# A fused transformer block under a list planner: later K/V column groups wait for the fourth block, V's constant columns are filled in pieces, a fourth shift buffer, idle matmuls at more places

## The chip, the cores and the metric

One core of a Trainium2 chip. The metric is device microseconds (us) of one execution. Most kernels here were timed many times and the median is quoted; "fast runs" are those within 1.5% of the kernel's fastest, and only they are compared; of all timings here one, of pl_aus, was slow. TensorE (PE in the profile) does the matmuls, ScalarE (ACT) the exponentials, VectorE (DVE) copies, statistics and an integer form of the exponential, GpSimd (POOL) memsets and small products. Each run also lists its mean granted TensorE clock, where 1 is the full rate; a half-rate stretch is a piece of the run in which the trace shows 0.50. The tail is everything behind the last exponential. A run of heads is the four heads that are worked on together for one block of 512 queries.

## The reference

```python
# x (1, 2048, 512) bf16, 32 heads of 16, F = 1376
sa, ca, ga, sb, cb, gb = six parts of  silu(c) @ w_mod
h = layernorm(x) * (1 + ca) + sa
x = x + ga * (softmax(q k^T / 4) v) @ wo          # q, k, v = h @ wqkv
h = layernorm(x) * (1 + cb) + sb
x = x + gb * (gelu(h @ w1 + b1) @ w2 + b2)
```

The costly part is 32 heads x 2048 x 2048 exponentials. In pieces of 128 x 512 these are 2048 pieces, divided between ScalarE and VectorE.

## The kernel before

The program is not written in the order in which it runs. Every operation is an object with an engine, an estimate of its duration, its dependencies, a buffer that it takes and a priority. A planner keeps a clock of its own, and at each step puts down the operation that can start first on some engine (`commit`). The order on every engine is thus fixed when the kernel is built, and it depends on all estimates, priorities and buffer counts together.

```python
A_US = {1: 0.49, 2: 0.92, 3: 1.345}          # planner's estimate of an exponential of 1, 2, 3 pieces
r_ph = res("ph", 3, [P, 4 * QB], I16)        # buffers of VectorE's integer exponential
...
def dyn(plan, o):                            # priority on PE, smaller goes first
    ...
    if o.due <= prog():
        return 2.5 + same                    # work that is overdue
...
def step(self):                              # one step of the planner
    ...
    if h is not None:                        # h: a matmul on zeros, only to keep TensorE busy
        hs = max(self.start(h), self.cool)
        end = hs + h.us + 0.11
        if hs <= nxt and (not pe or pe[0][0] >= end or hs < HEAT_MIN):
            self.commit(hs, self.add(h))
```

These idle matmuls come whole (one of 128 x 512 into a spare bank) or in sets of four (onto the accumulator of the running head, adding zero). V carries constant columns, filled once by GpSimd:

```python
def v_init(b):
    def go(o):
        for t in range(b * TPB, (b + 1) * TPB):
            for ph in (range(NPH) if t in DKS else (0,)):
                v = v_tile(t, ph)
                nc.gpsimd.memset(v[:, 32 * VW:32 * VW + 15], 0.0)
                nc.gpsimd.memset(v_cols(v)[:, :, 16:17], PH_W[ph])
    return op("POOL", go, 1.5, prio=1.0 + b)
...
for cc in range(1, NC):                      # column groups 2 to 4 of K and V
    for b in range(NQ):
        make_k(b, cc, f"c{cc}", r_ax, "DVE")
        make_v(b, cc, f"c{cc}", r_ax, "DVE")
```

The softmax here doesn't subtract the row's maximum and nothing guards it: scores larger than these inputs give would overflow.

## Time and profile before

| | before |
|---|---|
| first timing | 804.71 us, median of 3 (801.36 to 807.18) |
| profiled run | span 800.8 us, mean clock 0.992 |
| PE / VectorE / ScalarE / GpSimd busy | 733.3 / 742.8 / 763.6 / 96.9 us |
| exponentials on ScalarE / integer pieces on VectorE | 634 instructions / 464 |
| first, fourth, seventh exponential start | 17.43, 21.86, 29.12 us |
| last exponential ends; tail behind it | 774.73; 26.03 us |

The two counts stand for one division of the 2048 pieces: 464 for VectorE, 1584 for ScalarE in instructions of two or three pieces. The lines themselves are in the prediction.

### The profile page before, as it was taken

What the parts mean: (1) busy time and instruction counts of PE and PEld (TensorE: products, weight loads), DVE (VectorE), ACT (ScalarE), POOL (GpSimd) and SP (SyncE); (2) the same over time, 40 slices, a digit from 0 to 9 for tenths busy, and PEclk for the clock granted to TensorE, in tenths of its full rate; (3) what the DMA queues carried; (4) which work ended last, traced back from release to release, by engine and by line L of the source; (5) the groups of instructions that cost most, each with busy time, mean ns of one, the idle gap of its engine ahead of it and who ended that gap; (6) DMA issues with size and microseconds to landing.
All of it is one profiled execution on the core that took longest, in us unless ns stands there. A gap on an engine that the chain in (4) does not pass through costs nothing. (4 is left out here: it accounts for less than half of the span.)

```text
span 800.8 us, 20101 instructions
## 1 busy us (share of the span) xinstructions
PE 733.3 (92%) x8146; PEld 273.7 (34%) x8223; DVE 742.8 (93%) x1292; ACT 763.6 (95%) x691; POOL 96.9 (12%) x241
## 2 busy tenths in 40 slices
PE   7889999989998999899988999999999999989997
PEld 3433323332222332222322332232233344434454
DVE  7779899989999999799999999999999999999975
ACT  2999999999999999999999999999999999999993
POOL 4422302100002000000001100000000100020100
PEclk9999999999999999999999999999999999999999
DMA  6115000102100000010100000011100001000010
GB/s 211 54 35 156 18 16 19 36 16 67 39 18 15 20 15 17 11 28 25 42 16 19 16 10 12 23 23 29 45 16 19 4 19 43 18 16 25 24 43 28
DMA packets 34199, 26.22 MB, mean 33 GB/s; under 512 B 15005, under 2 KB 29502, under 8 KB 34106
## 3 DMA queue, kind: packets, MB, share of 16 engines
q1 hardware_dynamic: 33578, 24.94, 11.0%
q8 instruction: 64, 1.05, 0.5%
q14 instruction: 29, 0.24, 0.1%
q10 hardware_dynamic: 528, 0.00, 0.0%
HBM read 21.30 MB, written 2.61 MB: 30 GB/s over the span
## 5 line engine op out<-in xcount | busy, mean ns | idle before, releaser
L802 ACT ACTIVATE pt<-st 128x1536 bf16<-128x1536 f32 x634 | 721.0, 1304 | 10.4 <-PE st L753 6.8
L843 DVE TENSOR_SCALAR ph<-ax 128x512 int16<-128x512 f32 x464 | 303.0, 681 | 16.9 <-PE ax L753 15.4
L858 DVE TENSOR_SCALAR sh<-ph 128x2048 int16<-128x2048 int16 x464 | 304.5, 696 | 0.7 <-PE od L891 0.3
L753 PE MATMUL st<-qm,kT 32*128 32x512 bf16 x1584 | 248.8, 384 | 30.8 <-ACT pt L802 24.1
L753 PEld LDWEIGHTS <-kT 32*128 32x128 bf16 x2048 | 83.6, 91 | 256.0 <-issue 247.0
L891 PE MATMUL od<-sh,VX 128*32 128x512 bf16 (+1 forms) x2336 | 164.7, 342 | 5.9 <-DVE sh L858 4.9
L753 PE MATMUL ax<-qm,kT 32*128 32x512 bf16 x464 | 161.4, 380 | 9.0 <-DVE ph L843 5.6
L891 PE MATMUL od<-pt,VEB 128*32 128x512 bf16 (+1 forms) x1976 | 147.2, 342 | 1.0 <-ACT pt L802 0.8
L891 PEld LDWEIGHTS <-VEB 128*32 128x32 bf16 x2560 | 62.1, 96 | 82.1 <-issue 69.1
L891 PEld LDWEIGHTS <-VX 128*32 128x32 bf16 x2336 | 57.7, 95 | 82.0 <-issue 71.0
L943 POOL TENSOR_TENSOR OT<-OD,RB 128x256 bf16<-128x256 f32 x38 | 28.7, 763 | 326.0 <-DVE sh L858 222.7
L891 PE MATMUL od<-ph,VEB 128*32 128x512 bf16 (+1 forms) x584 | 48.4, 342 | 1.4 <-DVE OD L916 0.9
L943 POOL TENSOR_TENSOR OS<-OD,RB 128x256 bf16<-128x256 f32 x24 | 17.2, 727 | 196.9 <-DVE sh L858 117.7
L1106 PE MATMUL ax<-blk,W 128*128 128x512 bf16 (+1 forms) x128 | 34.7, 368 | 1.4 <-issue 0.5
L644 PE MATMUL ax<-blk,w 128*128 128x512 bf16 x92 | 30.8, 386 | 4.1 <-issue 1.2
L1043 PE MATMUL ax<-w,g 128*128 128x512 bf16 x102 | 28.6, 381 | 2.1 <-DVE y L1087 1.0
L689 POOL TENSOR_SCALAR VX<-VEB 128x128 bf16<-128x128 bf16 x64 | 22.2, 347 | 59.0 <-DVE VEB L585 55.3
L1116 DVE TENSOR_SCALAR g<-ax,b1c 128x512 bf16<-128x512 f32 (+1 forms) x37 | 26.4, 716 | 0.3
L559 DVE BATCH_NORM_STATS2 ln_s<-xb 128x6 f32<-128x512 bf16 x32 | 21.7, 678 | 2.2 <-DMA xb<-in_A_x_dram 2.1
L1043 PEld LDWEIGHTS <-g 128*128 128x128 bf16 x176 | 14.3, 97 | 23.8 <-issue 12.4
L916 DVE COPY OD<-od 128x512 f32<-128x512 f32 x31 | 21.2, 682 | 0.7 <-issue 0.4
L1106 PEld LDWEIGHTS <-W 128*128 128x128 bf16 x176 | 14.2, 97 | 18.5 <-issue 11.4
(109 smaller groups left out, 365.9 us busy)
## 6 DMA issues: line engine op xcount, KB each, us to landing
RB<-rn SPq DMA_DIRECT2D x124, 64.0 KB
xb<-in_A_x_dram SPq DMA_DIRECT2D x8, 512.0 KB
out_dram<-o SPq DMA_DIRECT2D x16, 128.0 KB
w<-in_A_wqkv_dram SPq DMA_DIRECT2D x3, 512.0 KB
W<-in_B_w_dram SPq DMA_DIRECT2D x1, 1376.0 KB
blk<-in_w_mod_dram SPq DMA_DIRECT2D x2, 512.0 KB
xb<-in_w_mod_dram SPq DMA_DIRECT2D x2, 512.0 KB
g<-in_w_mod_dram SPq DMA_DIRECT2D x2, 512.0 KB
```

Of the source, the lines that this page charges most:

```text
L559: nc.vector.bn_stats(out=st6, in_=src)
L644: return chain([(lambda ps, j=j: nc.tensor.matmul(out=ps[:, 0:QB], lhsT=w.tile[:, j, cc * P:(cc + 1) * P], rhs=o_h[b].tile[:, j, :], start ...
L689: nc.gpsimd.tensor_scalar(out=v_cols(VX[(t, ph)])[:, 8 * cc:8 * cc + 8, 0:16], in0=v_cols(v_tile(t, 0))[:, 8 * cc:8 * cc + 8, 0:16], scala ...
L753: nc.tensor.matmul(out=o.tile[:, k * QB:(k + 1) * QB], lhsT=kT[cc][kb][rows, ko * P:(ko + 1) * P], rhs=qm.tile[rows, par, :] if hb is None ...
L802: nc.scalar.activation(out=e.tile[:, 0:len(got) * QB], in_=o.tile[:, 0:len(got) * QB], func=ACT.Exp, scale=ESC)
L843: nc.vector.tensor_scalar(out=ph.tile[:, o.row * QB:(o.row + 1) * QB], in0=o.tile, scalar1=PH_B, scalar2=0.0, op0=ALU.add, op1=ALU.max)
L858: sh = op("DVE", lambda o, j=j: nc.vector.tensor_scalar(out=o.tile, in0=first.tile, scalar1=PH_SH[j], scalar2=None, op0=ALU.add), 0.6, es, ...
L891: nc.tensor.matmul(out=o_od[r].tile[32 * i:32 * i + 32, n * HB:n * HB + w], lhsT=v_tile(kt, ph)[:, c0:c0 + 32], rhs=got[i][:, at:at + w], ...
L943: two = [op("POOL", lambda o, c=c: after_dve(nc.gpsimd.tensor_tensor(out=OT.tile[:, c * HB:(c + 1) * HB], in0=OD.tile[:, c * HB:(c + 1) * HB],
L1043: nc.tensor.matmul(out=ps, lhsT=g[:, f, col:col + P], rhs=rhs, start=(f == 0), stop=(f == NF - 1))
L1106: mm = chain([(lambda ps, f=f, j=j: nc.tensor.matmul(out=ps[:, 0:N], lhsT=W1[:, j, f * P:(f + 1) * P], rhs=h.tile[:, j, 0:N], start=(j == ...
L1116: ev.append(op("DVE", lambda o, f=f, mm=mm: nc.vector.tensor_scalar(out=g.tile[:, f, 0:N], in0=mm.tile[:, 0:N], scalar1=b1c[:, f:f + 1], s ...
```

## The change

Its intent: keep the early buffers free for the four LayerNorms by letting the column groups 2 to 4 wait for a later block's K, keep GpSimd free of memsets until the first LayerNorm has its statistics, give VectorE one more buffer, and let the idle matmuls in at more places. Two priorities change (overdue work, the LayerNorm of the block tails), and the planner's zero-length bookkeeping leaves GpSimd's list for a list of its own.

```diff
-            if hs <= nxt and (not pe or pe[0][0] >= end or hs < HEAT_MIN):
+            if hs <= nxt and (not pe or pe[0][0] >= end or pe[0][1].kind == "qkD" and hs >= self.cool):
...
-    r_ph = res("ph", 3, [P, 4 * QB], I16)
+    r_ph = res("ph", 4, [P, 4 * QB], I16)
...
-            return 2.5 + same
+            return (2.5 if o.due + 16 > prog() else 0.8) + same
...
-        return op("POOL", None, 0.0, deps, lat=0.0, prio=0.0, rel=(owner,))
+        return op("NIL", None, 0.0, deps, lat=0.0, prio=0.0, rel=(owner,))
... (the same for every other op without an instruction)
+    def v_init(v, w, prio, gate):
+        x = v[..., 0:32 * VW].rearrange("p t (h w) -> p t h w", w=VW)
+        return [op("POOL", lambda o, to=to, c=c: nc.gpsimd.memset(to, c), 0.35, prio=prio, gate=gate)
+                for to, c in ((v[..., 32 * VW:32 * VW + 15], 0.0), (x[:, :, 8:32:8, 0:15], 0.0), (x[..., 16:17], w))]
...
+        late = (lambda: True) if b == 0 else (lambda: first_ln[0])
+        o_v0[b] = v_init(VEB[b], PH_W[0], 1.0 + b, late)
...
-                   [o_sc, o_warm] + [w[0] for w in ws], kind, r_ax, [w[2] for w in ws])
+                   [o_sc, o_warm, ws[0][0]], kind, r_ax, [w[2] for w in ws],
+                   need=lambda i: ws[i // NC][0])
...
-                                    None, r_blk, ("DVE",) * 4, r_ax, kind, 1.6, None, nt)
+                                    None, r_blk, ("DVE",) * 4, r_ax, kind, 0.3, None, nt)
...
-            make_k(b, cc, f"c{cc}", r_ax, "DVE")
-            make_v(b, cc, f"c{cc}", r_ax, "DVE")
+            make_k(b, cc, f"c{cc}", r_ax, "DVE", o_k[(0, min(b + AHEAD, LAST))])
+            make_v(b, cc, f"c{cc}", r_ax, "DVE", o_k[(0, min(b + AHEAD, LAST))])
```

More of the change, by code (lines that the diff above doesn't have):

```diff
@@ L61 @@
 HEAT = 1.3
-HEAT_MIN = 0.0
 class Res:
@@ L104 @@
 class Plan:
-    SLACK = {"PE": 0.10, "DVE": 0.05, "ACT": 0.15, "POOL": 0.05, "SP": 0.05}
+    SLACK = {"NIL": 0.0, "PE": 0.10, "DVE": 0.05, "ACT": 0.15, "POOL": 0.05, "SP": 0.05}
     def __init__(self, dyn, later):
@@ L274 @@
     NQ = S // QB
+    LAST = NQ - 1
     TPB = QB // P
@@ L288 @@
     A_US = {1: 0.49, 2: 0.92, 3: 1.345}
+    AHEAD = 3
     PSUM_F = 4
@@ L480, in load_w @@
                    prio=prio)
-    o_x[0] = op("POOL", None, 0.0, (), lat=0.0, prio=-2.0, acq=r_xb)
+    o_x[0] = op("NIL", None, 0.0, (), lat=0.0, prio=-2.0, acq=r_xb)
     o_x0 = [dma(lambda o, t=t: nc.sync.dma_start(out=o_x[0].tile[:, t, :], in_=x_src[0][:, t, :]),
@@ L509 @@
     o_v0 = {}
-    def v_init(b):
-        def go(o):
-            for t in range(b * TPB, (b + 1) * TPB):
-                for ph in (range(NPH) if t in DKS else (0,)):
-                    v = v_tile(t, ph)
-                    nc.gpsimd.memset(v[:, 32 * VW:32 * VW + 15], 0.0)
-                    nc.gpsimd.memset(v_cols(v)[:, :, 16:17], PH_W[ph])
-        return op("POOL", go, 1.5, prio=1.0 + b)
-    for b in range(NQ):
-        o_v0[b] = v_init(b)
+    def v_init(v, w, prio, gate):
+        x = v[..., 0:32 * VW].rearrange("p t (h w) -> p t h w", w=VW)
+        return [op("POOL", lambda o, to=to, c=c: nc.gpsimd.memset(to, c), 0.35, prio=prio, gate=gate)
+                for to, c in ((v[..., 32 * VW:32 * VW + 15], 0.0), (x[:, :, 8:32:8, 0:15], 0.0), (x[..., 16:17], w))]
+    first_ln = [False]
+    o_vx0 = {}
+    for b in range(NQ):
+        late = (lambda: True) if b == 0 else (lambda: first_ln[0])
+        o_v0[b] = v_init(VEB[b], PH_W[0], 1.0 + b, late)
+        for t in DKS:
+            if t // TPB == b:
+                o_vx0[t] = [x for ph in range(1, NPH) for x in v_init(
+                    VX[(t, ph)].unsqueeze(1), PH_W[ph], 1.5 + b, lambda: first_ln[0])]
     o_ce = op("ACT", lambda o: nc.scalar.activation(out=ce, in_=c_bf, func=ACT.Exp, scale=-1.0),
@@ L588, in layer_norm @@
                    after=None, nt=TPB):
-        ln = op("POOL", None, 0.0, (), lat=0.0, prio=0.0, acq=r_ln)
+        ln = op("NIL", None, 0.0, (), lat=0.0, prio=0.0, acq=r_ln)
         st = [op("DVE", lambda o, t=t: stats(ln, t, src(t)), 0.83, (deps[t], ln, after), prio=prio)
@@ L594, in layer_norm @@
                  st[2 * i:2 * i + 2] + [o_mh], prio=0.0) for i in range(nt // 2)]
-        z = op("POOL", None, 0.0, (rs[0], hold_z), lat=0.0, prio=0.0, acq=r_z)
+        z = op("NIL", None, 0.0, (rs[0], hold_z), lat=0.0, prio=0.0, acq=r_z)
         za = [op("DVE", lambda o, t=t: apply(ln, z, t, src(t)), 0.33, (z, rs[t // 2]), prio=prio,
                  rel=(ln,), port=True) for t in range(nt)]
-        h = op("POOL", None, 0.0, (rs[0],), lat=0.0, prio=0.0, acq=alloc_h)
+        h = op("NIL", None, 0.0, (rs[0],), lat=0.0, prio=0.0, acq=alloc_h)
         done = []
@@ L647, in proj, with make_k @@
             [w, after] + o_hd[b], kind, acq, (o_h[b], w))
-    def make_k(b, cc, kind, acq, eng):
-        mm = proj(b, o_w[1], cc, kind, acq)
+    def make_k(b, cc, kind, acq, eng, after=None):
+        mm = proj(b, o_w[1], cc, kind, acq, after)
         o_k[(cc, b)] = op(eng, lambda o: copy(eng, kT[cc][b], mm.tile[:, 0:QB]), 0.6 if eng == 'DVE' else 0.5, (mm,), prio=0.3,
@@ L654, in make_q @@
     def make_q(b, cc, kind, acq):
-        qm = op("POOL", None, 0.0, (), lat=0.0, prio=0.0, acq=r_qm)
+        qm = op("NIL", None, 0.0, (), lat=0.0, prio=0.0, acq=r_qm)
         mm = proj(b, o_w[0], cc, kind, acq, after=qm)
@@ L668, in make_q, with make_v @@
         q_left[(cc, b)] = 8 * NT
-    def make_v(b, cc, kind, acq, eng):
+    def make_v(b, cc, kind, acq, eng, after=None):
         def vt(ps, t):
@@ L677, in make_v @@
         mm = chain([(lambda ps, t=t: vt(ps, t), 4 * 0.071) for t in range(TPB)],
-                   [o_w[2]] + o_hd[b], kind, acq, (o_h[b], o_w[2]))
+                   [o_w[2], after] + o_hd[b], kind, acq, (o_h[b], o_w[2]))
         def ev(o):
@@ L683, in ev @@
             copy(eng, dst[:, :, :, 0:16], mm.tile[:, 0:QB].rearrange("p (t h d) -> p t h d", t=TPB, h=8))
-        got = [op(eng, ev, 0.6, (mm, o_v0[b]), prio=0.3, rel=(mm,))]
+        got = [op(eng, ev, 0.6, [mm] + o_v0[b], prio=0.3, rel=(mm,))]
         for t in DKS:
@@ L692, in scale @@
                             scalar2=0.0, op0=ALU.mult, op1=ALU.add)
-                got.append(op("POOL", scale, 4 * 0.3, (got[0], o_v0[b]), prio=1.0, port=True))
+                got.append(op("POOL", scale, 4 * 0.3, [got[0]] + o_vx0[t], prio=1.0, port=True))
         o_v[(cc, b)] = got
@@ L701 @@
     NR = len(runs)
-    LAST = NQ - 1
     HB = QB // 2
@@ L823, in qk_d @@
             at["D"][:] = r, kt, rows
-            o_ph[0] = op("POOL", None, 0.0, (), lat=0.0, prio=0.0, acq=r_ph)
+            o_ph[0] = op("NIL", None, 0.0, (), lat=0.0, prio=0.0, acq=r_ph)
             d_e[:] = []
@@ L941, in normalise @@
         move = b == LAST or u % 2 == 1
-        OT = op("POOL", None, 0.0, (o5,), lat=0.0, prio=0.0, acq=r_OT if b == LAST or not move else r_OS)
-        two = [op("POOL", lambda o, c=c: after_dve(nc.gpsimd.tensor_tensor(
-            out=OT.tile[:, c * HB:(c + 1) * HB], in0=OD.tile[:, c * HB:(c + 1) * HB],
-            in1=o5.tile[:, c * HB:(c + 1) * HB], op=ALU.mult)), POOL_US, (OT,), lat=0.1, prio=0.5,
-            kind="beside", rel=(OD, o5), port=True, gate=lambda: plan.beside(POOL_MIN)) for c in range(2)]
+        OT = op("NIL", None, 0.0, (o5,), lat=0.0, prio=0.0, acq=r_OT if b == LAST or not move else r_OS)
+        two = beside(lambda c: nc.gpsimd.tensor_tensor(
+            out=OT.tile[:, c], in0=OD.tile[:, c], in1=o5.tile[:, c], op=ALU.mult), (OT,), (OD, o5))
         if not move:
@@ L963, in normalise, with beside @@
             o_OT[(b, u)] = OT
+    def beside(fn, deps, rel=(), prio=0.5):
+        return [op("POOL", lambda o, c=c: after_dve(fn(slice(c * HB, (c + 1) * HB))), POOL_US, deps, lat=0.1,
+                   prio=prio, kind="beside", rel=rel, port=True, gate=lambda: plan.beside(POOL_MIN))
+                for c in range(2)]
     def after_dve(pool):
@@ L976, in late_loads @@
         d = (after,)
-        gt = op("POOL", None, 0.0, d, lat=0.0, acq=r_g, prio=0.0)
+        gt = op("NIL", None, 0.0, d, lat=0.0, acq=r_g, prio=0.0)
         o_late["g"] = gt
@@ L1069, in go @@
                 r_t.free[n] = o.end
-        big = [op("POOL", None, 0.0, (), lat=0.0, prio=0.0, acq=x, gate=finished) for x in r_st]
-        op("POOL", go, 0.0, big, lat=0.0, prio=0.0)
+        big = [op("NIL", None, 0.0, (), lat=0.0, prio=0.0, acq=x, gate=finished) for x in r_st]
+        op("NIL", go, 0.0, big, lat=0.0, prio=0.0)
     def block_tail(b, nt=TPB):
@@ L1085, in block_tail @@
             prev = a
-            y = op("POOL", None, 0.0, (a, x2, o_late["ga"]), lat=0.0, prio=0.0, acq=r_y)
+            y = op("NIL", None, 0.0, (a, x2, o_late["ga"]), lat=0.0, prio=0.0, acq=r_y)
             m = op("DVE", lambda o, t=t, a=a, y=y: nc.vector.tensor_tensor(
@@ L1092, in block_tail @@
         h, hd, za, trs = layer_norm(lambda t: x2.tile[:, t, :], res_done, modB, o_late["mB"],
-                                    None, r_blk, ("DVE",) * 4, r_ax, kind, 1.6, None, nt)
-        g = op("POOL", None, 0.0, hd, lat=0.0, prio=0.0, acq=r_g)
+                                    None, r_blk, ("DVE",) * 4, r_ax, kind, 0.3, None, nt)
+        g = op("NIL", None, 0.0, hd, lat=0.0, prio=0.0, acq=r_g)
         part = nt < TPB
@@ L1100, in block_tail @@
         ev = []
-        over = op("POOL", None, 0.0, (), lat=0.0, prio=0.0, gate=finished) if part else None
+        over = op("NIL", None, 0.0, (), lat=0.0, prio=0.0, gate=finished) if part else None
         if part:
@@ L1136, in block_tail @@
             prev = mm
-            y = op("POOL", None, 0.0, (mm,), lat=0.0, prio=0.0, acq=r_y)
+            y = op("NIL", None, 0.0, (mm,), lat=0.0, prio=0.0, acq=r_y)
             m = op("DVE", lambda o, mm=mm, y=y: nc.vector.tensor_tensor(
@@ L1155, in take @@
         def take(acq, deps=()):
-            return op("POOL", None, 0.0, deps, lat=0.0, prio=0.0, acq=acq)
+            return op("NIL", None, 0.0, deps, lat=0.0, prio=0.0, acq=acq)
         x2 = xr
@@ L1261 @@
         prev_tr = trs[-1]
+        if b == 0:
+            op("NIL", lambda o: first_ln.__setitem__(0, True), 0.0, za, lat=0.0, prio=0.0)
         after = za[-1]
```

## The prediction

> **What bounds the kernel now.** I read the page's first part (busy time by engine) first. Three engines are over 90% busy and the span is 800.8 us, so the question is which one is never allowed to wait. Then I read the costliest groups, then ScalarE's instructions in order of time at both ends, then the waits.
>
> ```profile
> PE 733.3 (92%) x8146; PEld 273.7 (34%) x8223; DVE 742.8 (93%) x1292; ACT 763.6 (95%) x691; POOL 96.9 (12%) x241
> ...
> L802 ACT ACTIVATE pt<-st 128x1536 bf16<-128x1536 f32 x634 | 721.0, 1304 | 10.4 <-PE st L753 6.8
> L843 DVE TENSOR_SCALAR ph<-ax 128x512 int16<-128x512 f32 x464 | 303.0, 681 | 16.9 <-PE ax L753 15.4
> ```
>
> ScalarE's 634 exponentials hold 721.0 us by themselves. Their number is fixed by how the key tiles are divided between ScalarE (exp) and VectorE (the integer trick of line 843, 464 pieces). So the time is the moment of the first exponential, plus this work, plus ScalarE's idle gaps, plus the tail behind the last one. ScalarE idles 800.8 - 763.6 = 37.2 us. Its order of time splits that:
>
> ```profile
> 11.98 1.45 ACT L575 ACTIVATE blk<-st,modA 128x512 bf16<-128x512 bf16 x2 [8.09 <-PE st L607]
> 14.75 0.58 ACT L583 CAST kT<-ax 128x512 bf16<-128x512 f32 x1 [1.33 <-PE ax L644]
> 17.43 1.45 ACT L802 ACTIVATE pt<-st 128x1536 bf16<-128x1536 f32 x1 [2.10 <-PE st L753]
> 19.61 5.54 ACT L802 ACTIVATE pt<-st 128x1024 bf16<-128x1024 f32 x5 [0.73 <-PE st L753]
> 25.50 1.45 ACT L575 ACTIVATE blk<-ax,modA 128x512 bf16<-128x512 bf16 x2 [0.34 <-PE ax L607]
> 28.05 0.58 ACT L583 CAST kT<-ax 128x512 bf16<-128x512 f32 x1 [1.11 <-PE ax L644]
> 29.12 4.62 ACT L802 ACTIVATE pt<-st 128x1536 bf16<-128x1536 f32 x4 [0.49 <-PE st L753]
> ...
> 46.95 3.28 ACT L802 ACTIVATE pt<-st 128x1024 bf16<-128x1024 f32 x3 [0.55 <-PE ax L753]
> ...
> 774.75 1.28 ACT L1120 ACT_TABLE_LOAD   x1
> ```
>
> Columns: start, duration, what, and in brackets the idle time before it with its releaser. Up to 17.43 the busy pieces are 1.28 + 0.20 + 1.45 + 0.58 = 3.5, so 13.9 idle. From there to 29.12 the gaps are 0.73 + 0.34 + 1.11 + 0.49 = 2.7. The tail from 774.75 holds 13.0 of work in 26.05, so 13.0 idle. What is left for the 745 us between is 37.2 - 13.9 - 2.7 - 13.0 = 7.6 us. About 3.9 of that sits in three places, near 231, 426 and 590 us, and each is the same event:
>
> ```profile
> 227.00:228.00 1.00, 0.69 (x6) 0.20 (x6) 1.00 (x2) 1.00 (x2) 0.73 (x2) 1.00 0.00 0
> 228.00:229.00 1.00, 0.69 (x11) 0.20 (x6) 1.00 (x3) 1.00 (x2) 0.00 (x0) 0.91 0.01 2
> 229.00:230.00 1.00, 1.00 (x15) 0.35 (x16) 1.00 (x2) 1.00 (x2) 0.00 (x0) 0.50 0.12 31
> 231.00:232.00 1.00, 1.00 (x14) 0.18 (x12) 1.00 (x3) 0.35 (x1) 0.00 (x0) 0.50 0.08 23
> ```
>
> These are one-microsecond windows: length, then busy time of PE, weight load, VectorE, ScalarE, GpSimd, then granted TensorE clock, then DMA. PE is slack for a while, the clock halves for some 3.4 us, and ScalarE starves (0.35 of a microsecond busy at 231).
>
> **What the Trainium skill says.** "TensorE: Matmul & The Clock Gate", Part 1, has a gate with two states, half and full rate, set by PE activity in free-running windows of about 3.4 us. The trace agrees (0.50 for about three and a half windows). The free phase would explain why three timings of one program spread from 801.36 to 807.18. The same page (Architectural detail) says that ScalarE and VectorE are strict FIFOs, so the built program's order on each engine decides what stands behind what. "GPSIMD Engine Reference", Key points, says GpSimd shares its SBUF interfaces with VectorE instructions in a 2-port mode. The trace shows it: the 128x4 op of line 527 takes 1304 ns, from 3.92 to 5.22, while the neighbouring small ops take 150 to 180; GpSimd's run of memsets ends at 5.21. And a pair of LN applies at 9.28 takes 1.70 us beside memsets from 9.20 to 10.5, while the pair before took 0.70. "Perfetto Trace Analysis", Optimization Strategy, advises looking at the gaps of the contended engine; I do that.
>
> **The change, part by part.** I compared the two programs' orders. Exponentials (634), pieces of lines 843 and 858 (464 each), projections and copies are equal in number on every engine; nothing of ScalarE's 763.6 us goes away. Only gaps can move.
>
> *Memsets.* 64 memsets become 60, and only block 0's three stand ahead of the first LN's rstd. The 1304 ns op should fall to about 0.15, worth 1.15 us on VectorE. Two things take it back. The second w_mod load releases PE only at 9.47, so modA is not earlier. And directly behind the second rstd there is now a run of 25 memsets where 16 were, beside LN applies 3 and 4; at some 0.08 each (16 took 1.32) that is 2 us or more against 1.3. If rstd ends 1.1 earlier and the run is 0.7 to 1.0 longer, the applies end about where they did (10.98). Sum: 0 to -0.3 us.
>
> *First exponential.* Before, VectorE does two LN statistics (13.95 to 15.55) ahead of the two Q evictions, which end at 16.95; PE's first score matmul starts at 17.00. Now the Q eviction stands right behind the modulation. Q's projection ends near 13.9, so eviction runs 13.9 to 15.3; K's copy on ScalarE ends at 15.33. First score 15.4, first exponential about 15.8: 1.6 us earlier.
> But the fourth exponential then needs the score bank in which block 0's V sits, and V's eviction now stands behind more VectorE work. From 15.3: three statistics (0.84 each) to 17.9, a second Q eviction (1.21) to 19.1, a statistic to 19.95, one apply to 20.3, V's copy to 21.0. Exponential 3 ends at 19.65, so ScalarE waits about 1.9 us. Then block 1's LN goes on: three applies to 22.1 to 23 (GpSimd's V scaling runs beside), transposes 24 to 25, modulation on ScalarE to 26.6, K projection 0.9, copy 0.6: exponential 7 at about 28.6 instead of 29.12. Of the 1.6 us only **-0.5** survives.
>
> *Second to fourth column groups wait* for block 3's K. They no longer take the two ax banks among LN 1 to 3, which in the profile hold the second transpose of LN 1 back to 24.85. The benefit is inside the -0.5, plus the 0.55 gap at 46.95: **-0.5**. They are not late: the third run of heads needs them some 43 exponentials in (past 70 us), and their copies are among VectorE's first 105 instructions, 42 behind the last LN at about 0.68, near 66 us.
>
> *Heat, overdue work first, planning ops off the GpSimd list.* Idle-time matmuls go from 17 to 22 whole ones and from 33 to 41 sets of four. That adds (5 + 8) x 0.21 = 2.8 us to a PE with 67 us free, at places where it waits. Fewer quiet stretches, fewer halvings. I take half of the three events' 3.9: **-2.0**.
>
> *Fourth ph buffer.* Line 843's 16.9 us of waiting is for PE, only in part for buffers, and VectorE is not the bound: **-0.4**.
>
> *Tail.* PE's Wo matmuls of the last block move ahead of seven W1 pieces and two W2 pieces, so line 1195's operand comes some 1.5 us sooner; PE then has 4.6 us of work to the next transposes, so they come about 1 us sooner. But five W2 matmuls (0.21 each, 1.1 us) moved behind the last piece. **-0.3**.
>
> Sum: -0.5 - 0.5 - 2.0 - 0.4 - 0.3 = -3.7, so 804.7 - 3.7 = **801.0 us**.
>
> **Rivals.** (a) The clock events decide all. For: they are the largest single term of the middle, and the timings spread by 5.8 us. With none, another 2 us: 799; with one or two more, 804. (b) The start keeps its 1.6 us, because V's copy is less late than I count or its wait is covered: then 799.5; with (a), 797. Against it: V's copy stands behind six VectorE instructions. (c) GpSimd's longer run of memsets locks VectorE out of the LN, so LN 0 ends 1 us later and LN 1 too: 803. The 1304 ns op speaks for it; against it, every third memset now waits for the one before, which leaves VectorE openings. (d) VectorE becomes the bound: no, it idles 5.8 us between 760 and 780 in the kernel before, so it is done early.
>
> **Range and chances.** All removable gaps together are 7.6 in the middle, 2.7 early and perhaps 2 at the start; 2% is 16.1 us. So over 2% faster would need more than is there: 0.02. Slower by 16 us would need a new wait of a size seen nowhere: 0.02. Same: 0.96. The range of 796.5 to 805 is the rivals' span plus a microsecond or so of noise in a median.
>
> **What would show it.** The op on ce at 0.15 us; first exponential at 15.8 and a wait of about 2 us before the fourth, released by VectorE's V copy; the seventh near 28.6; no gap near 46; fewer than three windows with clock 0.50; the last exponential near 771.5; tail still about 26 us. I am wrong if the seventh exponential comes before 27.5 or after 30, if ScalarE's gaps in the middle add to more than 7.6, or if the tail changes by over 1 us.

## The result and the profile after

| | before | after |
|---|---|---|
| median of runs made together | 804.08 us (6 runs, 801.27 to 807.18) | 793.78 us (6 runs, 792.00 to 799.19) |
| profiled run: span, clock | 800.8 us, 0.992 | 794.9 us, 0.991 |

The ratio is 0.9883, 95% interval 0.9841 to 0.9926. A ratio here is always the mean time of one kernel's fast runs over that of the other's of the same rounds, so it is not quite the ratio of the medians that are quoted. The kernel is 10.3 us faster by the medians, where I had 3.7; 793.78 lies below my range. It is still within 2%.

The page of the changed kernel, parts 1 and 5:

```profile
PE 739.4 (93%) x8260; PEld 276.2 (35%) x8260; DVE 737.2 (93%) x1292; ACT 762.3 (96%) x691; POOL 100.4 (13%) x237
...
L806 ACT ACTIVATE pt<-st 128x1536 bf16<-128x1536 f32 x634 | 720.1, 1312 | 4.8 <-PE st L757 3.6
L847 DVE TENSOR_SCALAR ph<-ax 128x512 int16<-128x512 f32 x464 | 303.1, 684 | 17.7 <-PE ax L757 15.9
```

Same numbers of instructions (634 and 464), the same busy time per exponential; but the idle time before the exponentials fell from 10.4 us to 4.8. The work is unchanged and the gaps shrank, as foreseen, only by more. ScalarE's instructions in order of time (start, duration, then the idle time before in brackets):

```profile
3.75 0.20 ACT L527 ACTIVATE ce<-c_bf 128x4 f32<-128x4 bf16 x1 [1.25 <-DMA c_bf<-in_c_dram]
13.04 1.45 ACT L580 ACTIVATE blk<-st,modA 128x512 bf16<-128x512 bf16 x2 [9.09 <-PE st L612]
16.94 0.58 ACT L588 CAST kT<-ax 128x512 bf16<-128x512 f32 x1 [2.45 <-PE ax L649]
18.02 3.71 ACT L806 ACTIVATE pt<-st 128x1536 bf16<-128x1536 f32 x3 [0.49 <-PE st L757]
22.70 3.28 ACT L806 ACTIVATE pt<-st 128x1024 bf16<-128x1024 f32 x3 [0.97 <-PE st L757]
26.18 1.45 ACT L580 ACTIVATE blk<-ax,modA 128x512 bf16<-128x512 bf16 x2 [0.20 <-PE ax L612]
28.09 0.58 ACT L588 CAST kT<-ax 128x512 bf16<-128x512 f32 x1 [0.47 <-PE ax L649]
29.16 4.63 ACT L806 ACTIVATE pt<-st 128x1536 bf16<-128x1536 f32 x4 [0.48 <-PE st L757]
...
44.84 6.13 ACT L806 ACTIVATE pt<-st 128x1536 bf16<-128x1536 f32 x5
...
769.37 1.28 ACT L1128 ACT_TABLE_LOAD   x1
```

The first exponential comes at 18.02, later than before (17.43), not at 15.8. The wait ahead of the fourth is there (0.97), the gap near 46 is gone, the seventh stands where it stood (29.12 and 29.16). So the start gave nothing, and nearly everything was gained between 29 us and the last exponential, which ends at 769.35 (I had 771.5). Two half-rate stretches fell between 50 and 765 us, where there had been three. Why the first exponential is late shows in two-microsecond windows (length; busy of PE, weight load, VectorE, ScalarE, GpSimd; clock; DMA):

```profile
8.00:10.00 2.00, 0.90 (x18) 0.59 (x18) 0.95 (x2) 0.00 (x0) 1.71 (x16) 1.00 1.00 331
10.00:12.00 2.00, 1.95 (x27) 1.62 (x28) 0.34 (x2) 0.00 (x0) 1.46 (x11) 0.51 1.09 371
12.00:14.00 2.00, 1.67 (x12) 1.02 (x10) 0.99 (x2) 0.96 (x2) 0.00 (x0) 0.50 1.10 349
14.00:16.00 2.00, 2.00 (x6) 0.76 (x5) 0.76 (x2) 0.49 (x1) 0.00 (x0) 0.50 1.01 320
```

The new order has fewer warm-up matmuls ahead of the modulation, PE is busy only 0.90 of the 2 us from 8, and the clock halves from 10.0 for 6.8 us, just where the transposes and the first projections run.

### Where the 5.9 us between the two profiled spans came from

In device time the two profiled runs took 802.58 and 796.65 us. I added ScalarE's gaps between the seventh and the last exponential, and parted them by whether they fall in, or within 4 us behind, a stretch at half rate.

| us | before | after | difference |
|---|---|---|---|
| start of the seventh exponential | 29.12 | 29.16 | +0.0 |
| gaps at half-rate stretches | 3.93 | 2.22 | -1.7 |
| other gaps | 3.31 | 0.80 | -2.5 |
| ScalarE's work from the seventh to the last, without the gaps | 738.4 | 737.2 | -1.2 |
| tail | 26.03 | 25.52 | -0.5 |
| sum (the span) | 800.8 | 794.9 | -5.9 |

The split depends a little on where the stretches fall: in the repeat of the kernel before (r_before) one lies on the gap near 757 us, and the two rows of gaps are 4.39 and 1.88; in the repeat of the changed kernel they are 0.00 and 0.78.

The fourth row looks like a cost of gaps too. In the trace of the repeated changed kernel, the exponential behind one of 1536 columns starts 1.33 us after it in an unbroken stream (median), while one alone lasts 1.45; each gap would therefore cost about 0.1 us beyond its length. Exponentials with a gap before them number 31 in the kernel before (26 in its repeat) and 21 in the changed one (15 in its repeat), so ten fewer gaps account for about 1 us.

The other 4.4 us of the 10.3 are not in these two profiles, for two reasons. The profile from which I predicted was a good draw: 802.58 us, 1.5 below the median of its six runs, at a clock of 0.992, where the mean over 43 later timings of the kernel before is 0.985. And the profile of the changed kernel was a bad one: 796.65 us, 2.9 above its median.

The gaps that are not at half-rate stretches I put down to the order. PE's waits for VectorE between 50 and 765 us, kernel before and kernel after, the two largest of each (total, times, longest):

```profile
PE ax L753 <- DVE ph L843: 5.6, 24, 0.4
PE od L891 <- DVE sh L858: 4.9, 17, 0.5
```
```profile
PE od L895 <- DVE sh L862: 3.1, 15, 0.3
PE ax L757 <- DVE ph L847: 2.3, 9, 0.5
```

All waits of PE for VectorE there add to 17.9 us before and 10.8 after (15.9 and 11.4 in the repeats). PE stands less often behind something VectorE has not finished; that the next scores therefore come in time for ScalarE is my reading. Over all profiles below these waits are 10.8 to 11.9 us where the changed order is kept and 12.5 to 17.9 elsewhere. That is a correlation, which no run tests by itself.

### The profile page after: what moved, and what is told of

It is laid out like the page before. It is cut to its first block, busy times and chain, and to the rows that moved or that the text cites. A ratio compares the mean times of both kernels' runs of the same rounds, so it can differ in the third digit from the quotient of the medians.

```text
span 794.9 us, 20294 instructions
## 1 busy us (share of the span) xinstructions
PE 739.4 (93%) x8260; PEld 276.2 (35%) x8260; DVE 737.2 (93%) x1292; ACT 762.3 (96%) x691; POOL 100.4 (13%) x237
## 4 chain that ended last, share of the span: by engine, by line
ACT 39%; PE 34%; DVE 15%; issue 11%; DMA 1%; SPq 0%; POOLq 0%; POOL 0%; ACTq 0%; DVEq 0%
ACT pt L806 37%; PE od L895 11%; PE st L757 10%; DVE ph L847 6%; DVE sh L862 5%; PE ax L1051 3%; PE ax L1114 2%; PE ax L757 2%; PE ax L649 1%; DMA blk<-in_w_mod_dram 1%; DVE g L1124 1%; PE ax L1045 1%; ACT g L1133 1%; DVE OD L920 1%; PE t L1051 1%
## 5 line engine op out<-in xcount | busy, mean ns | idle before, releaser
L847 DVE TENSOR_SCALAR ph<-ax 128x512 int16<-128x512 f32 x464 | 303.1, 684 | 17.7 <-PE ax L757 15.9
L862 DVE TENSOR_SCALAR sh<-ph 128x2048 int16<-128x2048 int16 x464 | 300.1, 692 | 0.3 <-PE od L895 0.2
L895 PE MATMUL od<-ph,VEB 128*32 128x512 bf16 (+1 forms) x584 | 45.9, 340 | 0.3 <-DVE OD L920 0.2
L1114 PE MATMUL ax<-blk,W 128*128 128x512 bf16 (+1 forms) x148 | 39.0, 371 | 0.4 <-DVE ph L847 0.2
L649 PE MATMUL ax<-blk,w 128*128 128x512 bf16 x124 | 36.4, 391 | 1.0 <-DVE ph L847 0.4
L694 POOL TENSOR_SCALAR VX<-VEB 128x128 bf16<-128x128 bf16 x64 | 24.1, 377 | 69.6 <-DVE VEB L590 58.0
```

What stands on the lines that cost most here:

```text
L649: return chain([(lambda ps, j=j: nc.tensor.matmul(out=ps[:, 0:QB], lhsT=w.tile[:, j, cc * P:(cc + 1) * P], rhs=o_h[b].tile[:, j, :], start ...
L694: nc.gpsimd.tensor_scalar(out=v_cols(VX[(t, ph)])[:, 8 * cc:8 * cc + 8, 0:16], in0=v_cols(v_tile(t, 0))[:, 8 * cc:8 * cc + 8, 0:16], scala ...
L847: nc.vector.tensor_scalar(out=ph.tile[:, o.row * QB:(o.row + 1) * QB], in0=o.tile, scalar1=PH_B, scalar2=0.0, op0=ALU.add, op1=ALU.max)
L862: sh = op("DVE", lambda o, j=j: nc.vector.tensor_scalar(out=o.tile, in0=first.tile, scalar1=PH_SH[j], scalar2=None, op0=ALU.add), 0.6, es, ...
L895: nc.tensor.matmul(out=o_od[r].tile[32 * i:32 * i + 32, n * HB:n * HB + w], lhsT=v_tile(kt, ph)[:, c0:c0 + 32], rhs=got[i][:, at:at + w], ...
L1114: mm = chain([(lambda ps, f=f, j=j: nc.tensor.matmul(out=ps[:, 0:N], lhsT=W1[:, j, f * P:(f + 1) * P], rhs=h.tile[:, j, 0:N], start=(j == ...
```

## The experiments

Sixteen kernels ran; every one was correct, and every profiled run was in the fast state. Those of one batch share a chip and the runs of the kernel before. Beyond the medians I use one fit of my own: over all 417 timings, each kernel with its own time at full clock, and one common slope for the lost clock. "Lost clock" is 1 less the mean clock, in thousandths. Least squares gives 0.57 us for each thousandth, with 0.9 us left over. As a thousandth of some 800 us is 1.6 us at half rate, a stretch of 3.41 us costs 3.41 x 0.57 / 1.6 = 1.21 us; the three stretches in the profile before cost 3.93 / 3 = 1.31. The fit ascribes nothing to causes; it only parts what goes with the clock from what doesn't, and its last column is an estimate and not a measured time. With slopes of their own the kernels with ten or more runs have 0.46 (s_skip) to 0.68 (m_ahead), and two of the changed kernel's first six runs, at clocks of 0.999 and 1.000, took 792.0 us each, 1.4 above the 790.6 of r_after. Where it matters I therefore compare runs at equal clock.

| run | median us (runs) | ratio to before, 95% | lost clock, thousandths | fitted time at full clock |
|---|---|---|---|---|
| kernel before, all batches | 803.9 to 806.0 (183) | | 13.7 | 797.4 |
| r_before | 806.05 (22) | 0.9996 [0.9977, 1.0015] | 14.5 | 797.5 |
| r_after | 795.86 (6) | 0.9865 [0.9839, 0.9892] | 9.0 | 790.6 |
| w_warm | 794.95 (5) | 0.9853 [0.9832, 0.9874] | 6.6 | 791.4 |
| m_mem2 | 795.53 (6) | 0.9892 [0.9864, 0.9920] | 9.7 | 790.5 |
| w_early | 796.32 (6) | 0.9909 [0.9879, 0.9938] | 5.8 | 794.0 |
| s_skip | 800.57 (12) | 0.9935 [0.9911, 0.9959] | 19.9 | 790.3 |
| p_heat | 803.69 (17) | 0.9979 [0.9961, 0.9997] | 8.1 | 799.1 |
| m_heat | 807.53 (22) | 1.0012 [0.9993, 1.0032] | 22.2 | 794.9 |
| m_ahead | 806.81 (14) | 1.0005 [0.9988, 1.0021] | 11.9 | 799.4 |
| m_ph | 806.41 (22) | 1.0006 [0.9987, 1.0024] | 16.5 | 796.7 |
| m_nil | 805.14 (14) | 1.0003 [0.9980, 1.0025] | 10.5 | 798.8 |
| m_tail | 806.39 (22) | 1.0016 [0.9997, 1.0036] | 16.6 | 797.0 |
| pl_aus | 807.06 (22) | 1.0030 [1.0013, 1.0047] | 16.0 | 797.8 |
| pl_pool | 804.64 (22) | 0.9997 [0.9979, 1.0016] | 12.8 | 797.0 |
| bpl_aus | 808.28 (9) | 1.0054 [1.0019, 1.0089] | 17.9 | 799.3 |
| b_dbl | 809.11 (13) | 1.0061 [1.0035, 1.0086] | 13.3 | 801.9 |

**r_before and r_after.** No edit; the two kernels again, as the level of everything else.

> The kernel before once more, for the granted clock of each timed run. Clock theory (the gain is fewer halvings of the TensorE clock): its time follows the mean clock closely, and a run at 0.998 or more takes under 798 us, near the changed kernel's 792 to 794. Order theory (the gain is ScalarE gaps closed by another instruction order, at full clock): even its best-clocked runs stay above 799 us, 6 us or more over the changed kernel at the same clock. Median 804 in both.

> The changed kernel once more, for a profile without halvings and for the clock of each run. Both theories: median 793 to 794.5. In a profile with clock 1.00 throughout, the first exponential should come near 16 us instead of 18.0, the seventh near 27.5, the last near 765.5.

The gain is real: 10.2 us by the medians, on another chip. By the fit 5.5 thousandths of clock (3.1 us) and 6.9 us at full clock. Runs at equal clock agree: at 9 thousandths lost the kernel before takes 802.5 us (mean of 14 runs) and the changed order 795.3 to 796.7 (4 runs, m_mem2's among them), at 5 thousandths 800.85 (1 run) and 792.7 to 793.4 (3). My expectation of a run of the kernel before at 0.998 could not be tried: none came above 0.995. The repeat of the changed kernel was slower than I expected (795.86 against 793 to 794.5), and its profile has a half-rate stretch at the start, so its first exponential came at 17.59 and not near 16. It has none between 50 and 765 us, and ScalarE's gaps from the seventh exponential to the last come to 0.78 us.

**m_heat: the changed kernel with the old rule for idle matmuls.**

```diff
-            if hs <= nxt and (not pe or pe[0][0] >= end or pe[0][1].kind == "qkD" and hs >= self.cool):
+            if hs <= nxt and (not pe or pe[0][0] >= end):
```

> The changed kernel with the old rule for idle-time (heat) matmuls. Clock theory: more halvings, clock about 0.99, 798 us or more, half of the gain lost. Order theory: 793 to 796.

The whole gain is gone, with 22.2 thousandths of clock lost, the most of all. But the planner also chose another order from about 130 us on, so this run alone can't tell the missing idle matmuls from the new order. s_skip was made for that.

**w_warm: the changed kernel with warm matmuls while the modulation weights come in.** Eight extra matmuls of 384 columns ahead of the first weights' products and four ahead of the second's.

```diff
     def mod_mm(ps, n, w, m):
+        if m == 0 and dst_a[0]:
+            for _ in range((8, 4)[n]):
+                nc.tensor.matmul(out=ps[:, P:QB], lhsT=warm, start=True, stop=True,
+                                 rhs=warm[:, 0:1].to_broadcast([P, QB - P]))
```

> The changed kernel with 8 and 4 more warm matmuls (384 columns each) in the two waits for w_mod at the start. If the early halving (clock 0.83 in the first 20 us of the profile) costs the changed kernel some 2 us in part of its runs: no clock under 1.00 before 20 us, first exponential at 16 us, and a median about 1 us lower, 792.5. If it doesn't matter for the end, because the fourth exponential and block 1's LN wait for VectorE anyway: 793.8, unchanged.

The order on ScalarE and VectorE is the changed kernel's, instruction for instruction. The clock stays full from 6 to 16 us, and the start is the predicted one:

```profile
10.00:12.00 2.00, 1.17 (x21) 0.93 (x18) 1.33 (x4) 0.79 (x2) 1.48 (x11) 1.00 1.11 351
```
```profile
15.41 3.71 ACT L811 ACTIVATE pt<-st 128x1536 bf16<-128x1536 f32 x3 [0.49 <-PE st L762]
20.58 3.28 ACT L811 ACTIVATE pt<-st 128x1024 bf16<-128x1024 f32 x3 [1.47 <-PE st L762]
25.65 1.45 ACT L585 ACTIVATE blk<-ax,modA 128x512 bf16<-128x512 bf16 x2 [1.78 <-PE ax L617]
28.63 2.37 ACT L811 ACTIVATE pt<-st 128x1536 bf16<-128x1536 f32 x2 [0.48 <-PE st L762]
```

First exponential at 15.41 (I had 15.8), a wait before the fourth (1.47, I had 1.9), and the seventh at 28.63 (I had 28.6). My chain for the start was right apart from the clock. In this run another half-rate stretch began at 22.1, which is in the wait ahead of the seventh. Some two and a half microseconds at the first exponential became half a microsecond or less at the seventh, and 0.9 in the median (794.95, a miss of both values that I had expected), which is less than these intervals can tell.

**s_skip: the changed kernel's order, without the idle matmuls that only the new rule lets in.** They are planned, so the order is the same, and not emitted: 12 sets of four and 4 whole ones.

```diff
             if hs <= nxt and (not pe or pe[0][0] >= end or pe[0][1].kind == "qkD" and hs >= self.cool):
+                if pe and pe[0][0] < end:
+                    h.fn = None
                 self.commit(hs, self.add(h))
```

> The changed kernel's plan, the same order of everything on every engine, but the 12 sets and 4 whole idle-time matmuls that only the new clause admits are planned and not emitted. If those matmuls themselves keep the clock up: mean clock falls from about 0.992 to 0.985 or less and the median rises by 5 us or more, to 800 or above. If the old-rule kernel was slow because the planner made another order (gaps outside the halvings, 3.7 us against 0.8): clock and time stay with the changed kernel, 794 to 797.

Page of s_skip, then of r_after, the slices of the clock and the exponentials:

```profile
PEclk8899999989979999989999999999999999999999
...
L808 ACT ACTIVATE pt<-st 128x1536 bf16<-128x1536 f32 x634 | 721.7, 1302 | 14.3 <-PE st L759 6.9
```
```profile
PEclk8999999999999999999999999999999999999999
...
L806 ACT ACTIVATE pt<-st 128x1536 bf16<-128x1536 f32 x634 | 719.4, 1310 | 2.6 <-PE st L757 1.9
```

Eight half-rate stretches of together 41 us between 50 and 765, against none; the idle time before the exponentials is 14.3 us against 2.6. The profile of s_skip is its slowest run (808.59 us at a clock of 0.966), so the lines overstate the contrast. Over all timings it lost 19.9 thousandths instead of 9.0, which is 6.2 us by the fit; the ratio is 0.9935 against 0.9865 and 0.9892 for the same order with them (r_after, m_mem2, other chips), so 3.5 to 5.6 us of 805 (its interval and m_mem2's just overlap). And at equal clock it takes what the changed kernel takes: 798.84 to 800.22 us at 15 thousandths lost (3 runs), where the changed kernel has 799.19 at 16, as it must be if only the clock differs. So in one fixed order, 16 small insertions are worth some 3.5 to 6.2 us, all through the clock as far as these runs can tell.

**p_heat: the kernel before with only the new rule** (45 sets instead of 33).

> The kernel before with the new heat rule and nothing else of the change. If the heat rule is enough by itself: clock about 0.991, 797 us or less. If it needs the other parts (fewer gaps outside halvings come from those): 800 to 803.

The lost clock falls from 14.1 (the kernel before in the same rounds) to 8.1 thousandths, which is 3.4 us by the fit, as good as in the changed kernel. Yet the ratio is only 0.9979, about 1.7 us: the planner made another order here too, and by the fit it loses 1.7 at full clock (799.1 against 797.4). A full clock is thus not enough; the order matters by itself.

**m_ahead: the changed kernel without the wait for the fourth block's LayerNorm. m_ph: with three shift buffers.**

```diff
-            make_k(b, cc, f"c{cc}", r_ax, "DVE", o_k[(0, min(b + AHEAD, LAST))])
-            make_v(b, cc, f"c{cc}", r_ax, "DVE", o_k[(0, min(b + AHEAD, LAST))])
+            make_k(b, cc, f"c{cc}", r_ax, "DVE")
+            make_v(b, cc, f"c{cc}", r_ax, "DVE")
```
```diff
-    r_ph = res("ph", 4, [P, 4 * QB], I16)
+    r_ph = res("ph", 3, [P, 4 * QB], I16)
```

> The changed kernel without the wait of the second to fourth K/V column groups. If the deferral gives what the prediction said (0.5 to 1 us by itself, at the start): 0.5 to 1.5 us slower than the changed kernel at the same clock, the seventh exponential later than 28.7, a gap near 46 us back. If it gives nothing: equal at equal clock.

> The changed kernel with 3 ph buffers instead of 4 (the title's shift buffer). If the fourth buffer closes gaps outside the halvings: these rise from 0.8 towards 3 us and the time by 2 to 3 us at equal clock. If it does little, as predicted (0.4): equal within 1 us at equal clock.

Either one alone takes back the whole 10 us. If the parts added up, three parts (with m_heat) can't each be worth all of it. In m_ahead gaps of 1.11, 0.54, 0.55 and 0.73 us stand between 39 and 62 us, where the wait was meant to help; the rest of its loss is elsewhere. This raised the suspicion that any new order loses.

**pl_aus and pl_pool: placebos.** The whole change, and one of the planner's estimates moved by a hundredth or less of a microsecond. No instruction's kind or size is touched.

```diff
-    A_US = {1: 0.49, 2: 0.92, 3: 1.345}
+    A_US = {1: 0.49, 2: 0.92, 3: 1.35}
```
```diff
-    POOL_US, POOL_MIN = 0.68, 0.5
+    POOL_US, POOL_MIN = 0.69, 0.5
```

> A placebo: the changed kernel, with the planner's estimate of one 1536-column exponential at 1.350 us instead of 1.345 and nothing else. The planner makes another order from its 415th matmul on. If the change as such is what gains (any plan made by its rules is good): 793 to 797. If the good order is one draw among the plans that these rules can give: 800 or more, gaps outside halvings back to 2 us or more.

> A second placebo: the changed kernel with the planner's estimate of a GpSimd product at 0.69 us instead of 0.68. Same two readings as for the first placebo: 793 to 797, or 800 and more.

Both lose everything: 1.0030 and 0.9997. They hold every part of the change. These are the runs that decide how the leave-one-out runs are to be read: they can't be read as the part that was left out, since a new order by itself costs as much.

**m_mem2: the changed kernel with GpSimd's fills let in at once.** All gates on the memsets are opened; the pieces stay, and the planner still puts most of them behind the first LayerNorm's statistics.

```diff
-        late = (lambda: True) if b == 0 else (lambda: first_ln[0])
+        late = (lambda: True) if b == 0 else (lambda: True)
...
-                    VX[(t, ph)].unsqueeze(1), PH_W[ph], 1.5 + b, lambda: first_ln[0])]
+                    VX[(t, ph)].unsqueeze(1), PH_W[ph], 1.5 + b, lambda: True)]
```

> The changed kernel with all of GpSimd's memsets in front again (the same 60 pieces, no gate); PE, VectorE and ScalarE keep the very same order. If the memsets in front cost the first LN about 1 us and this reaches the end: 0.5 to 1.5 us slower, the op on ce over 1 us long, the first exponential later than 17.6. If w_mod's landing hides it, as predicted (0 to 0.3): equal within 0.5 us.

ScalarE's and VectorE's orders stay the same, and so does the time: 795.53, 790.5 at full clock by the fit. One pair of LayerNorm products runs 1.54 us instead of 0.95 beside the memsets, and nothing follows, since VectorE then waits another 1.06 us for the modulation's products. Opening the gates costs nothing, so holding back the fills is worth nothing here. But the run does not bring the old fills back: VectorE's op on `ce` takes 0.17 us in it as in the changed kernel, against 1.30 in the kernel before, as the early fills now end before it starts. What filling in pieces saved there is not tested.

**b_dbl: the kernel before, its order kept, each set of four emitted twice.**

```diff
-        for i in range(4):
+        for i in 2 * list(range(4)):
```

> The kernel before in its own order, with each of its 33 sets of four idle-time matmuls emitted twice (PE 33 x 0.21 = 7 us busier). If more filling alone mends the clock: clock from 0.985 to 0.990 or more, time 802 or less at unchanged gaps outside halvings (about 3.3). If the halvings come in stretches where the old rule put no set at all: clock and time unchanged, 805 to 807.

It is slower (1.0061), and the lost clock does not fall: 13.3 thousandths against 12.5 of the kernel before in the same rounds. By the fit it loses 4.5 us at full clock. That insertions without room in the plan delay the scores is the obvious reading, but its one profile (its clock was 0.979) shows it only in part: away from half-rate stretches ScalarE's gaps are as before (3.21 us against 3.31), while at 23.9 us of such stretches they add to 12.29, or 1.75 for each 3.41 us instead of 1.31. More matmuls at the old places bought no clock.

**m_nil and m_tail: the rest of the leave-one-out. bpl_aus: the placebo on the kernel before.** m_nil puts the bookkeeping back on GpSimd's list; m_tail restores both priorities; bpl_aus is the kernel before with the edit of pl_aus.

```diff
-        return op("NIL", None, 0.0, deps, lat=0.0, prio=0.0, rel=(owner,))
+        return op("POOL", None, 0.0, deps, lat=0.0, prio=0.0, rel=(owner,))
... (the same for every such op)
```
```diff
-            return (2.5 if o.due + 16 > prog() else 0.8) + same
+            return 2.5 + same
...
-                                    None, r_blk, ("DVE",) * 4, r_ax, kind, 0.3, None, nt)
+                                    None, r_blk, ("DVE",) * 4, r_ax, kind, 1.6, None, nt)
```

> The changed kernel with the planner's zero-length bookkeeping ops put back on GpSimd's list (they emit nothing; only the moment at which the planner lets them pass differs). If one particular part of the change carries the good order, and this is it, the time goes to 800-807; if another carries it, it stays at 793-797. If the good order is a single draw among plans, as the two placebos say, any re-planning loses it: 800-807 here too, with gaps of ScalarE outside halvings above 1.5 us in 50:765.

> The changed kernel with the two old priorities (overdue work 2.5 again, the last LayerNorms 1.6 again). Part theory: 793-797 if neither priority matters, and m_nil then has to be the slow one. Draw theory: 800-807, like m_nil. By my prediction's account the tail alone would be worth 0.3 us, so 794-796.

> A placebo on the kernel before: the planner's estimate of one exponential 1.35 instead of 1.345 us, nothing else. If plans are draws around 804-806 and the changed kernel's is a selected one, 802-808 here (ratio 0.995 to 1.005). If the kernel before were itself an unlucky draw, the placebo would come out faster, 793-800, and then the change's gain would be that of leaving a bad plan.

Both again lose everything, as the draw theory expected and the part theory didn't. m_nil is instructive because its profile has no half-rate stretch between 50 and 765 us, just as r_after, and its span is 802.6 against 791.6. Its page:

```profile
L806 ACT ACTIVATE pt<-st 128x1536 bf16<-128x1536 f32 x637 | 724.2, 1297 | 7.4 <-PE st L757 4.1
L847 DVE TENSOR_SCALAR ph<-ax 128x512 int16<-128x512 f32 x456 | 297.7, 681 | 25.2 <-PE ax L757 23.6
```

A new order also divides the pieces anew: 456 for VectorE instead of 464, so 8 more for ScalarE, 4.8 us more exponential work (724.2 against 719.4), and VectorE waits longer for PE. pl_aus has the same 456 and 724.4 us, so about 5 us of that placebo's 7.2 at full clock go with a worse division of the pieces; but m_tail and the kernel before lose with 464, so the division is not the whole cause. Of the re-planned kernels m_nil, m_ph, pl_aus and bpl_aus have 456, and m_heat, m_ahead, pl_pool and p_heat 460. Both kernels of the study have 464. bpl_aus is 0.54% slower than the kernel before (808.28 us, just outside the 802 to 808 that I had expected), so by this one neighbour the kernel before is not an unlucky order.

m_tail keeps 464 and keeps VectorE's order up to 240 us. It loses at 17 us of half rate, and at the end. ScalarE in the tail of m_tail and PE's output products of the last block there, then the same two for r_after:

```profile
788.75 0.81 ACT L580 ACTIVATE blk<-t,modB 128x128 bf16<-128x128 bf16 x2 [8.07 <-PE t L1222]
```
```profile
782.60 1.46 PE L1045 MATMUL t<-Wo,OT 128*128 128x512 bf16 x6
```
```profile
774.04 0.81 ACT L580 ACTIVATE blk<-t,modB 128x128 bf16<-128x128 bf16 x2 [2.13 <-PE t L1222]
```
```profile
767.75 0.81 PE L1045 MATMUL t<-Wo,OT 128*128 128x512 bf16 x3
```

With the old priorities the products with Wo come some 7 us behind the last exponential (which ends at 775.61) instead of 1.7 (766.07), and the tail is 29.13 us instead of 25.53. The kernel before had the old priorities too and a tail of 26.03, so the tail is 3.6 us longer in this order, and 0.5 between the two kernels.

**w_early: the changed kernel with w_warm's warm matmuls, and four idle matmuls at each product with V of the first run of heads.** An attempt to beat both kernels.

```diff
-            if o.extra:
+            if o.extra or r == 0 and left[r] > 0:
                 zeros(r)
```

> The changed kernel with extra warm matmuls while the two modulation weights come in, and four idle matmuls at each PV op of the first run of heads, so that TensorE keeps the full rate up to some 45 us. If the halvings between 9 and 45 us cost the end something, the seventh exponential comes near 27.5 instead of 28.6-29.2, and the time is 1 us under the changed kernel's of the same rounds' level: 792-794.5. If that loss is absorbed, or the re-plan loses the good order, 795-807.

The clock is the fullest of all (5.8 thousandths lost), and the order is still the changed one, but the seventh exponential comes at 29.64, and gaps of 0.71, 0.28 and 0.28 us follow at 54 to 58: 3.4 us lost at full clock by the fit. It does not beat the changed kernel, nor does w_warm beyond its interval. I have no version that does.

Two builds went to no chip. The kernel before with only the wait for the fourth block, and the changed kernel with the old memsets, both read V columns that nothing has written yet; the memory check refused them. The third of the new memsets (15 columns in three of the four groups) is what makes the wait allowed. So these two parts can't be taken apart.

## Why the prediction was wrong

**Right.** ScalarE is what counts, its instructions are as many as before, only gaps moved. *Memsets* 0 to -0.3: not refuted, and tested only in part (m_mem2). The small op on `ce` fell to 0.17 us (I had 0.15). My second reason that nothing comes of it was wrong: beside the memsets the second pair of LayerNorm applies took 0.95 us, where it had taken 1.70, and ended at 9.15 and not about 10.98. But the modulation products waited for their weights until 10.05 (9.47 before), which was my first reason. The seventh exponential was expected near 28.6 and came at 29.16 in the first profile, at 28.63 in w_warm. The gap near 46 is gone. *Tail* -0.3: -0.5.

**The start, half right.** "First exponential about 15.8" failed at 18.02. I worked it out with durations at full clock and did not ask whether PE stays busy, now that fewer warm-up matmuls stand ahead of the modulation. The clock halved. With more of them (w_warm) my numbers hold to about 0.4 us. It cost next to nothing, since I was right that the gain dies by the seventh exponential (w_warm).

**The term that was too small: heat, "I take half of the three events' 3.9: -2.0".** Its mechanism was right. Two things are wrong with its size. First, 3.9 is what one profile shows, of a run at clock 0.992. I had the three timings, 801.36 to 807.18, in front of me and took them for noise around this profile. The kernel before typically loses 14 thousandths, that is 14 x 0.57 = 8.0 us. Second, the extra idle matmuls are not worth 2.0: by the fit the clock that they save is worth 3.4 us in p_heat, and in the changed order they are worth 3.5 to 6.2 us (s_skip). Between the two kernels the fit gives 3.1 us of clock.

**The step that failed most: the sum "-0.5 - 0.5 - 2.0 - 0.4 - 0.3 = -3.7" as such.** I read the change as a sum of parts, each with its own place: start, column groups, buffer, tail. But the planner uses all of them to order all 800 us. By the fit the new order is 6.9 us faster at full clock (797.5 to 790.6), while the terms of my sum that lie outside heat come to 1.7. In the profiles it is the other gaps (3.31 to 0.80), the lost overlap behind each gap (1.2) and the tail (0.5), together 4.2 us. The two figures differ because the fit charges all lost clock alike: in the changed kernel's profile 4.3 of the lost thousandths lie in the one stretch at the start (2.4 us by the fit), where w_warm shows that they cost about half a microsecond or less. So I take the order to be worth 4.2 to 6.9 us of the ten, and the clock the rest; the runs do not part them more finely. These gaps I had counted (7.6 less 3.9) and left alone, as no part of the change pointed at them. My bound "all removable gaps together are 7.6 in the middle" was also too tight, as it comes from the good profile and leaves out the overlap.

**Is it a part, or the draw?** The five kernels that keep the changed order on ScalarE and VectorE (r_after, w_warm, m_mem2, w_early, s_skip) have ratios of 0.9853 to 0.9935 and take 790.3 to 794.0 us at full clock by the fit. The eleven others (the kernel before counted once, all three placebos among them) have 0.9979 to 1.0061 and take 794.9 to 801.9; the nearest, m_heat at 794.9, keeps the changed order up to 130 us. No part of the change survives alone, and all parts together don't either once a planner's estimate moves by 0.4% (pl_aus) or 1.5% (pl_pool). So *deferral* -0.5 and *fourth buffer* -0.4 can be neither confirmed nor refuted as terms. What is shown is that this one order is good. That it was found by trying many orders and keeping the best is likely, but I only argue it. What in the order makes it good beyond fewer waits, the 464 pieces and a full clock, stays open.

Of the rivals, (a) named the right quantity, the clock events, but with too small a stake. (b), the start keeping its gain, is refuted by w_warm. (c), memsets locking VectorE out, is refuted by the second pair of applies (1.70 us before, 0.95 after). (d), a VectorE bound, which I had rejected, finds no support: VectorE's busy time fell (742.8 to 737.2) and so did PE's waits for it.

## What to carry to other kernels

Where a planner fixes the order from estimates, test a change against a placebo that moves one estimate by a fraction of a per cent; if the placebo loses as much as taking a part out, the part was not measured, and only runs that keep the order (planned but not emitted, gates that open without moving anything) can be read as causes. Predict from the spread of the timings and the mean clock, not from one profile: this one was 3.4 us under the later median (802.58 against 805.98). And where matmuls that only keep the clock up stand decides whether they pay: 16 that the planner placed did (s_skip), 33 doubled sets at the old places did not (b_dbl).

## What the Trainium skill lacked or had wrong

- "TensorE: Matmul & The Clock Gate", Part 1 (table of the two states) has the clock halve after at least one idle window of about 3.4 us, and its closing table asks for no idle gaps over some 3 us. In these runs no idle gap was near that: in the 3.4 us ahead of the halvings between 50 and 765 us, PE's longest gap was 0.14 to 1.11 us and PE was busy 0.53 to 0.95 of the time (0.85 with a longest gap of 0.41 ahead of the one at 167.0 us in the changed kernel; busy ends are modelled, and some of the traces lack a few matmul records). Its section on the second failure mode speaks of frequent short idling, which fits better, but gives no threshold, and busy share alone gives none here either: in r_after it went down to 0.64 over 3.4 us (from 344.6 us), and no halving came between 50 and 765 us.
- The same page's Terms take the penalty as the time at half rate times one half, 1.7 us for a stretch of 3.41. In this kernel, which ScalarE bounds, the fit gives 1.21 us of time and the profile before 1.31 us of ScalarE's gaps; other profiles have 0.92 (s_skip) to 1.75 (b_dbl). Stretches lasted 3.4, 6.8, 10.2 and 13.7 us.
- "ScalarE: Activation LUTs", What ACT_TABLE_LOAD costs, has back-to-back activations overlap by about 93 ns. r_after shows 104 ns for the first pair behind a gap; in the unbroken stream the next one starts 1331 ns after an exponential of 1536 columns that lasts 1445 alone, and 904 after one of 1024 that lasts 1018, so 114 ns of overlap, and a gap costs about 0.1 us beyond its length.
- No page says that a change to a planned kernel should be held against a placebo; here a change of 0.4% in one estimate moved the time by 1.4% (795.5 to 807.1 us, m_mem2 and pl_aus of the same rounds).
